# Loading the gate and up weights of a mixed decode kernel at the begin instead of the end

## The chip, the cores and the metric

The kernel runs on one core of one Trainium2 chip. The metric is device time in microseconds (us), the median of several runs. TensorE (PE) multiplies matrices and transposes, VectorE (DVE) and ScalarE (ACT) move and transform tiles, GpSimd (POOL) prepares constants, and SyncE (SP) issues nearly all of the DMAs.

## The reference

One decode step for four sequences, with two branches that a gate mixes:

```python
x = A_x                                                       # (4, 1, 512)
g = sigmoid((x * gate_w).sum(-1, keepdims=True))
# branch A: attention, 32 query heads, 8 key/value heads, head size 128, last 4096 positions
q = (x @ wq) as (4, 32, 1, 128)
scores = einsum("bhqd,bhkd->bhqk", q, k) * 128 ** -0.5        # k, v: last 4096 of 16384 positions
a = einsum("bhqk,bhkd->bhqd", softmax(scores), v) as (4, 1, 4096) @ wo
# branch B: a gated feed-forward of width 1792
gate = x @ W_gate;  up = x @ W_up
h = relu(gate) * up
b = h @ W_down
out = g * a + (1 - g) * b
```

Everything large is bf16. Per run the core reads 81.01 MB from HBM, almost all of it the windows of the key and value caches; the result is 4 KB.

## The kernel before

The attention is cut into `NSET = 8` sets; a set is one sequence and four of its eight key/value heads. Each set needs one block of keys (4096 KB, 32 KB in each of 128 partitions) and one block of values of the same size. `Ksb` and `Vsb` each have two slots, used in turn by even and odd sets. `Wbig` is a third buffer of 32 KB per partition.

Every engine's instructions are written down in order in a `Program`, with named events; a wait on an event becomes a semaphore wait ahead of the instruction. The order on each engine is thus set by hand, and nothing is rescheduled. SP's list is the order of the DMAs (lines 217 to 243). All are on SP's one queue, and the blocks land in the order of issue. A DMA that reuses a slot waits on SP until the last reader of the slot has finished, and everything behind it on SP waits too:

- wq into slot 1 of `Vsb` (line 533, issued ahead of the block), then K0, K1, V0, K2, V1, ..., K7, V6. K of set s waits for the scores of set s-2 (`SC`), V of set s for the products with V of set s-2 (`PV`; V1, into wq's slot, for an idle round).
- W_gate and W_up (1792 KB each, lines 230 and 232) into slot 0 of `Ksb`, which wait for the scores of set 6, the last reader of that slot. Then V7, which waits for `PV` of set 5.
- W_down (line 235) into slot 0 of `Vsb`, which waits for `PV` of set 6. Then wo into `Wbig` in five pieces (lines 240 and 243: 2048, 1280, 512 and twice 128 KB), with no wait of their own.

x and gate_w are small and come on ACT's queue (lines 224, 225).

PE's list: x is transposed (292), the gate's sum made (299), q = x @ wq (310) turned (328) and copied. A hardware loop then goes four times over two sets each. For a set, 64 transposes of K blocks (352) go through PSUM tile `TRT`; DVE (359) and ACT (357) copy them back over K. After five of the eight groups of transposes come the first half of the scores (373), after the rest the second half; DVE adds a mask and keeps the maximum (383). Then come the 64 products with V of the *previous* set (421), whose exponent (403, ACT) and transposition (413, DVE) ran beside this set's transposes.

Behind the loop stands the tail: the last set's maximum (390), exponent and transposition; `combine(0)` (440 to 448), which normalises the even sets; `gateup()` (453 to 474), that is 32 matmuls of x with W_gate and W_up into `TRT`, a ReLU on ACT and three operations on DVE, which make `hT`; the last set's 64 products with V; `combine(1)`; then 28 products of `hT` with W_down and 64 with wo, all accumulated in one PSUM tile (503), in the order in which the pieces of wo land; two copies (517, 518) and the DMA of the result (539).

## Time and profile before

| what | before |
|---|---|
| median of 3 runs | 196.43 us (196.17 to 196.50) |
| the profiled execution's own time | 196.16 us |
| its span in the profile | 194.9 us |
| bytes from HBM | 81.01 MB, 416 GB/s over the span |
| busy PE, PEld, DVE, ACT, POOL | 129.2, 101.0, 73.8, 66.5, 11.7 us |
| mean granted TensorE clock | 0.939 |

The profile is one execution, in microseconds from the span's start; 1.26 us of that execution lie outside the span. PE is TensorE's matmuls, PEld its weight loads, "SPq" the DMA issues of SP. L352 is line 352 of the kernel before. A timeline row gives start, duration, engine, line and operation, output<-input, count, and in brackets the idle time ahead of it with what ended it. A chain row gives start, duration, what. In rows with stretches of time, each engine's busy time and count is followed by the granted clock (1.00 is full), the busy share of the 16 DMA engines and GB/s.

### The profile page before, as it was taken

The numbers are of one execution on the slowest core, as the hardware profiler recorded it, in microseconds if no ns is written. First come the engines' busy times: TensorE is split into PE (matmuls) and PEld (weight loads), VectorE is DVE, ScalarE is ACT, GpSimd is POOL, SyncE is SP. The second block draws the span as 40 slices with busy tenths as digits, with TensorE's granted clock in tenths as the row PEclk, the third lists the DMA queues.
The fourth block names the chain that finished last, engine by engine and source line by source line (L and its number), as shares of the span: only waits on it lengthen the run. The fifth ranks groups of instructions, "written<-read, shape, count | busy, mean of one in ns | idle before, by whom it ended". The sixth has DMA issues, their size and how long they took to land.

```text
span 194.9 us, 3496 instructions
## 1 busy us (share of the span) xinstructions
PE 129.2 (66%) x1578; PEld 101.0 (52%) x1578; DVE 73.8 (38%) x95; ACT 66.5 (34%) x77; POOL 11.7 (6%) x43
## 2 busy tenths in 40 slices
PE   0137398788769649872887099649972987713964
PEld 0113396576556439651765097439651865503742
DVE  0200045259239323930682029324920492180000
ACT  2005025565255452435342424433435252510000
POOL 8820000000000000000000000000000000000000
PEclk9999999999999996999999859996999699995799
DMA  6999999999999999999999999999999999998992
GB/s 216 431 430 437 430 430 427 437 440 430 437 440 430 437 430 437 430 430 437 432 437 425 430 437 430 430 437 430 430 430 430 430 390 427 475 430 382 424 403 82
DMA packets 3881, 81.11 MB, mean 416 GB/s; under 512 B 409, under 2 KB 930, under 8 KB 1058
## 3 DMA queue, kind: packets, MB, share of 16 engines
q1 hardware_dynamic: 3864, 81.01, 97.3%
q8 instruction: 5, 0.08, 0.2%
q14 instruction: 2, 0.02, 0.0%
q10 hardware_dynamic: 10, 0.01, 0.0%
HBM read 81.01 MB, written 0.00 MB: 416 GB/s over the span
## 4 chain that ended last, share of the span: by engine, by line
DMA 59%; PE 21%; DVE 14%; ACT 3%; issue 1%; SPq 1%
DMA Ksb<-in_A_k_cache_dram 47%; PE TRT L352 15%; DMA Wbig<-in_A_wo_dram 12%; DVE Ksb L359 6%; DVE pT L413 5%; PE SCT L373 3%; DVE sc L383 3%; ACT Ksb L357 3%; PE OB L421 2%; PE SCT L503 1%; SPq L240 0%; PE FB L390 0%; SPq L533 0%; ACT outr L518 0%; SPq L235 0%
## 5 line engine op out<-in xcount | busy, mean ns | idle before, releaser
L352 PE MATMUL TRT<-identw,Ksb 128*128 128x128 f32 x512 | 75.1, 306 | 25.4 <-DMA Ksb<-in_A_k_cache_dram 17.5
L352 PEld LDWEIGHTS TRT<-identw,Ksb 128*128 128x128 f32 x512 | 65.9, 158 | 35.8 <-DMA Ksb<-in_A_k_cache_dram 18.8
L357 ACT COPY Ksb<-TRT 128x1024 f32<-128x1024 f32 x40 | 40.5, 1012 | 58.4 <-PE TRT L352 58.2
L359 DVE COPY Ksb<-TRT 128x1024 f32<-128x1024 f32 x24 | 29.4, 1223 | 40.1 <-PE TRT L352 40.1
L421 PE MATMUL OB<-Vsb,pT 128*32 128x256 bf16 x576 | 19.0, 288 | 7.5 <-DMA Vsb<-in_A_v_cache_dram 7.5
L373 PE MATMUL SCT<-Ksb,qS 128*32 128x512 bf16 x256 | 16.9, 381 | 8.8 <-ACT Ksb L357 8.8
L421 PEld LDWEIGHTS OB<-Vsb,pT 128*32 128x32 bf16 x576 | 16.4, 101 | 10.4 <-issue 7.9
L383 DVE CUSTOM_DVE_ANT_0 sc<-SCT,mask,mx 128x1024 bf16<-128x1024 f32 x8 | 10.3, 1284 | 26.9 <-PE SCT L373 26.9
L403 ACT ACTIVATE sc<-sc,negmax 128x2048 bf16<-128x2048 bf16 x8 | 16.0, 2002 | 10.7 <-DVE negmax L395 10.7
L413 DVE STREAM_TRANSPOSE pT<-sc 128x2048 bf16<-128x2048 bf16 x8 | 18.4, 2302 | 2.2 <-ACT sc L403 2.2
L430 ACT COPY osb<-OB 128x256 f32<-128x256 f32 x8 | 3.0, 372 | 31.1 <-PE OB L421 31.1
L373 PEld LDWEIGHTS SCT<-Ksb,qS 128*32 128x32 bf16 x256 | 5.2, 94 | 15.7 <-ACT Ksb L357 11.6
L383 DVE CUSTOM_DVE_ANT_0 sc<-SCT,mask 128x1024 bf16<-128x1024 f32 x8 | 9.8, 1225 | 2.2 <-PE SCT L373 2.2
L340 POOL COPY qS<-qW 128x64 bf16<-128x64 bf16 x8 | 1.8, 238 | 113.3 <-PE SCT L373 105.2
L390 PE MATMUL FB<-identw,mx 128*128 128x128 f32 x18 | 4.7, 343 | 5.7 <-issue 5.7
L395 DVE CUSTOM_DVE_ANT_0 mrow<-FB,qmask 128x128 f32<-128x128 f32 x8 | 2.3, 292 | 12.8 <-PE FB L390 12.8
L390 PEld LDWEIGHTS FB<-identw,mx 128*128 128x128 f32 x18 | 2.9, 200 | 7.6 <-issue 7.6
L292 PE MATMUL FB<-identw,xw 5*128 5x5 f32 x4 | 0.6, 262 | 8.5 <-POOL m L267 8.5
L503 PE MATMUL SCT<-Wbig,oq 128*4 128x256 bf16 x64 | 4.3, 273 | 2.6 <-DMA Wbig<-in_A_wo_dram 2.6
L310 PE MATMUL SCT<-Vsb,xT 128*32 128x512 bf16 x32 | 3.6, 631 | 2.8 <-DMA Vsb<-in_A_wq_dram 2.8
L292 PEld LDWEIGHTS FB<-identw,xw 5*128 5x128 f32 x4 | 0.6, 207 | 8.5 <-DVE xw L286 8.5
L503 PEld LDWEIGHTS SCT<-Wbig,oq 128*4 128x4 bf16 x64 | 2.7, 87 | 4.2 <-DMA Wbig<-in_A_wo_dram 3.6
(61 smaller groups left out, 42.7 us busy)
## 6 DMA issues: line engine op xcount, KB each, us to landing
Ksb<-in_A_k_cache_dram SPq DMA_DIRECT2D x8, 4096.0 KB, 24.2
Vsb<-in_A_v_cache_dram SPq DMA_DIRECT2D x8, 4096.0 KB, 32.2
Vsb<-in_A_wq_dram SPq DMA_DIRECT2D x1, 4096.0 KB, 12.3
Wbig<-in_A_wo_dram SPq DMA_DIRECT2D x1, 2048.0 KB, 21.5
Ksb<-in_B_W_gate_dram SPq DMA_DIRECT2D x1, 1792.0 KB, 19.7
Ksb<-in_B_W_up_dram SPq DMA_DIRECT2D x1, 1792.0 KB, 23.6
Vsb<-in_B_W_down_dram SPq DMA_DIRECT2D x1, 1792.0 KB, 17.0
Wbig<-in_A_wo_dram SPq DMA_DIRECT2D x1, 1280.0 KB, 24.1
```

Of the source, the lines that this page charges most:

```text
L310: P.op("pe", lambda e, half=half, t=t, g=g, col=col: e.matmul(SCT[32 * g:32 * g + 32, 512 * half:512 * half + 512], xT[:, t, :], Wq3[:, t, ...
L352: P.op("pe", lambda e, bk=bk, cc=cc, c=c: e.transpose(bk[:, cc * 128:(cc + 1) * 128], Kw[:, s % 2, c * 128:(c + 1) * 128], identw[:, :]), ...
L357: P.op("act", lambda e: e.copy(dst, bk), ("KTC", s, i), [("KT", s, i)], sem="va")
L359: P.op("dve", lambda e: e.tensor_copy(dst, bk), ("KTC", s, i), [("KT", s, i)], sem="vd")
L373: P.op("pe", lambda e, a=a, o=o, hb=hb, bank=bank: e.matmul(SCT[32 * a:32 * a + 32, 512 * hb:512 * hb + 512], qS[:, s % 2, o, :], k4[:, 16 ...
L383: P.op("dve", lambda e: e.tensor_tensor_reduce(sc[:, s % 2, pair * 1024:(pair + 1) * 1024], SCT[:, :], mask[:, :], 1.0, mx[:, s % 2, 0:1] ...
L390: P.op("pe", lambda e: e.matmul(FB[:, 384:512], mx[:, par, 1:2].to_broadcast([128, 128]), identw[:, :], start=True, stop=True), ("MT", s), ...
L403: P.op("act", lambda e: e.activation(sc[:, par, :], sc[:, par, :], ACTF.Exp, bias=negmax[:, par:par + 1], scale=SCALE, accum_out=rowsum[:, ...
L413: P.op("dve", lambda e: e.transpose(pT[:, par, :], sc[:, par, :]), ("PTT", s), [("EXP", s), ("PV", s - 2) if s >= 1 else None], sem="vd")
L421: P.op("pe", lambda e, g=g, blk=blk: e.matmul(OB[32 * g:32 * g + 32, 0:256], pT[:, par, 32 * blk:32 * blk + 32], Vsb[:, par, 256 * blk:256 ...
L430: P.op("act", lambda e: e.copy(osb[:, s, :], OB[:, 0:256]), ("OSB", s), [("PV", s)], sem="va")
L503: P.op("pe", lambda e: e.matmul(AB[32 * u:32 * u + 4, 0:256], stat, mov[:, 256 * u:256 * u + 256], start=start, stop=stop, tile_position=( ...
```

## The change

W_gate and W_up now go into `Wbig`, and wo into slot 0 of `Ksb`; `Wg`, `Wu` and `Wo3` name the new places.

- DMA order: W_gate takes the place ahead of the block that wq had, on a semaphore of its own; then come W_up, wq, K0, K1, V0 and so on. At the end V7 follows V6 directly, then W_down and the five pieces of wo. The pieces of wo have the scores of set 6 to wait for, an event that comes before the `PV` of set 6 for which W_down ahead of them waits.
- The 32 matmuls and four other operations of `gateup()` are written ahead of x @ wq, with W_gate's and W_up's waits separate. The first matmul of the loop's maximum waits for `hT` instead of x's transpose, and PE waits before the loop for the ReLU and the product, since the loop writes `TRT`.

Operations, sizes and pieces are the same.

```diff
-        Wg = Ksb[:, 0, 0:4 * FF].rearrange("p (t f) -> p t f", t=4)
-        Wu = Ksb[:, 0, 4 * FF:8 * FF].rearrange("p (t f) -> p t f", t=4)
+        Wg = Wbig[:, 0:4 * FF].rearrange("p (t f) -> p t f", t=4)
+        Wu = Wbig[:, 4 * FF:8 * FF].rearrange("p (t f) -> p t f", t=4)
...
-        Wo3 = Wbig[:, :].rearrange("p (i w) -> p i w", w=512)
+        Wo3 = Ksb[:, 0, :].rearrange("p (i w) -> p i w", w=512)
...
-        P.events[("V", -1)] = ("V1", 16, None, 0)
+        P.events[("WG",)] = ("wg", 16, None, 0)
...
+        P.dma("sp", lambda e: e.dma_start(Wbig[:, 4 * FF:8 * FF], B_W_up.rearrange("(p t) f -> p (t f)", p=128)), ("WU",))
+        P.dma("sp", lambda e: e.dma_start(Vsb[:, 1, :], A_wq.rearrange("(p t) w -> p (t w)", p=128)), ("V", -1), sem="V1")
         load_k(0)
         for s in range(1, NSET):
             load_k(s)
             load_v(s - 1)
-        P.dma("sp", lambda e: e.dma_start(Ksb[:, 0, 0:4 * FF], B_W_gate.rearrange("(p t) f -> p (t f)", p=128)),
-              ("WG",), [("SC", NSET - 2, NPAIR - 1)])
-        P.dma("sp", lambda e: e.dma_start(Ksb[:, 0, 4 * FF:8 * FF], B_W_up.rearrange("(p t) f -> p (t f)", p=128)),
-              ("WU",), [("SC", NSET - 2, NPAIR - 1)])
         load_v(NSET - 1)
...
-            P.dma("sp", lambda e, lo=lo, hi=hi: e.dma_start(Wbig[:, lo:hi], wo_src[:, lo:hi]), ("WO", k))
+            P.dma("sp", lambda e, lo=lo, hi=hi: e.dma_start(Ksb[:, 0, lo:hi], wo_src[:, lo:hi]), ("WO", k), [("SC", NSET - 2, 1)])
...
-                                                   wo_src3[:, WO_CUTS[-1]:32, 256 * u:256 * u + 256]), ("WOL", u))
+                                                   wo_src3[:, WO_CUTS[-1]:32, 256 * u:256 * u + 256]), ("WOL", u), [("SC", NSET - 2, 1)])
...
+        for t in range(4):
+            for which, W in ((0, Wg), (1, Wu)):
+                for g in range(4):
+                    P.op("pe", lambda e, which=which, W=W, t=t, g=g: e.matmul(
+                        TRT[32 * g:32 * g + 32, 512 * which:512 * which + FQ], xT[:, t, :], W[:, t, FQ * g:FQ * g + FQ],
+                        start=(t == 0), stop=(t == 3), tile_position=(0, 32 * g)),
+                        ("GU", which) if (t == 3 and g == 3) else None,
+                        [("WG",) if which == 0 else ("WU",), ("XTC",)])
...
-                 ("MT", s), [("SCC", s, 1)] if s >= 0 else [("XTC",)])
+                 ("MT", s), [("SCC", s, 1)] if s >= 0 else [("H",)])
...
-        def gateup():
...
+        P.op("pe", None, None, [("H0",), ("H1",)])
         for s in range(NSET):
...
         combine(0)
-        gateup()
         values(NSET - 1)
...
-        nc.sync.dma_start(Vsb[:, 1, :], A_wq.rearrange("(p t) w -> p (t w)", p=128)).then_inc(sems["V1"], 16)
+        nc.sync.dma_start(Wbig[:, 0:4 * FF], B_W_gate.rearrange("(p t) f -> p (t f)", p=128)).then_inc(sems["wg"], 16)
```

36 lines of the change are left out of this document (14 added, 22 removed).

## The prediction, made before the changed kernel was run

> **What bounds the kernel now.** I read the page's slices first, for the resource that is never idle:
>
> ```profile
> DMA  6999999999999999999999999999999999998992
> GB/s 216 431 430 437 430 430 427 437 440 430 437 440 430 437 430 437 430 430 437 432 437 425 430 437 430 430 437 430 430 430 430 430 390 427 475 430 382 424 403 82
> q1 hardware_dynamic: 3864, 81.01, 97.3%
> ```
>
> The 16 DMA engines are busy from the first slice (4.87 us each) to the last but one, at about 430 GB/s; the queue of the loads takes 97.3% of the span. The time is that of 81.01 MB in one queue, plus a head and a tail. Then the chain that ended last, for what follows the stream:
>
> ```profile
> 86.43 25.15 DMA Ksb<-in_A_k_cache_dram
> ...
> 126.19 24.25 DMA Ksb<-in_A_k_cache_dram
> ...
> 163.98 1.78 PE OB L421 x49
> ...
> 165.77 0.33 SPq L235
> ...
> 166.62 24.15 DMA Wbig<-in_A_wo_dram
> 190.81 2.38 PE SCT L503 x32
> ```
>
> K6 comes from 86.43+25.15 = 111.58, K7 from 150.44. The chain names W_down's and wo's issues (165.77, 166.14) because it goes back by semaphores; whether they were late is told by the backlog ahead of them. SP's timeline has the issues:
>
> ```profile
> 0.81 0.41 SPq L533 DMA_DIRECT2D Vsb<-in_A_wq_dram  x1
> ...
> 37.36 0.54 SPq L217 DMA_DIRECT2D Ksb<-in_A_k_cache_dram  x1
> ...
> 144.80 0.34 SPq L230 DMA_DIRECT2D Ksb<-in_B_W_gate_dram  x1
> 145.18 0.43 SPq L232 DMA_DIRECT2D Ksb<-in_B_W_up_dram  x1
> 146.54 0.55 SPq L221 DMA_DIRECT2D Vsb<-in_A_v_cache_dram  x1
> 165.77 0.33 SPq L235 DMA_DIRECT2D Vsb<-in_B_W_down_dram  x1
> 166.14 1.38 SPq L240 DMA_DIRECT2D Wbig<-in_A_wo_dram  x3
> ...
> 193.60 0.35 SPq L539 DMA_DIRECT2D out_dram<-outr  x1
> ```
>
> And the timeline of the compute engines from K7's landing on, to the last products:
>
> ```profile
> 150.48 5.42 PE L352 MATMUL TRT<-identw,Ksb 128*128 128x128 f32 x32 [3.57 <-DMA Ksb<-in_A_k_cache_dram]
> ...
> 163.81 1.92 PE L421 MATMUL OB<-Vsb,pT 128*32 128x256 bf16 x64
> ...
> 169.39 1.70 PE L457 MATMUL TRT<-Ksb,xT 128*32 128x448 bf16 x32
> ...
> 170.00 2.31 DVE L413 STREAM_TRANSPOSE pT<-sc 128x2048 bf16<-128x2048 bf16 x1 [2.16 <-ACT sc L403]
> 170.95 0.54 ACT L464 ACTIVATE hrelu<-TRT 128x448 f32<-128x448 f32 x1 [0.98 <-PE TRT L457]
> ...
> 172.81 0.89 DVE L466 TENSOR_TENSOR hrow<-TRT,hrelu 128x448 f32<-128x448 f32 x1
> ...
> 174.41 0.22 DVE L470 TENSOR_TENSOR hT<-hcol,gsb 128x56 bf16<-128x56 f32 x1
> ...
> 178.59 3.60 PE L421 MATMUL OB<-Vsb,pT 128*32 128x256 bf16 x64 [7.50 <-DMA Vsb<-in_A_v_cache_dram]
> ...
> 184.62 1.69 PE L503 MATMUL SCT<-Vsb,hT 128*4 128x256 bf16 x28
> ...
> 185.14 0.29 DVE L448 TENSOR_TENSOR oq<-TRT,rgate 64x128 bf16<-64x128 f32 x1
> 187.70 1.92 PE L503 MATMUL SCT<-Wbig,oq 128*4 128x256 bf16 x32 [1.39 <-DMA Wbig<-in_A_wo_dram]
> 190.81 2.37 PE L503 MATMUL SCT<-Wbig,oq 128*4 128x256 bf16 x32 [1.19 <-DMA Wbig<-in_A_wo_dram]
> ```
>
> To see: in the tail PE waits for each block of the stream in turn: V7 at 178.59, wo's first piece at 187.70, its second at 190.81. The last 32 products need 1.92 us (as the 32 before them did) and lie over 2.37: 0.45 us in them are waits for the last pieces. The end is set by the stream's last landing.
>
> **The change part by part.** *The same bytes in another order.* No DMA is added or removed. W_gate and W_up, 3584 KB = 3.67 MB, go from behind V6 to the front: at 430 GB/s all from wq to V6 lands 8.5 us later, and V7, W_down and wo, with the same bytes ahead of them as before, land when they did. In the sum: 0, if the queue never runs dry. The start stays as it is: the first issue is at 0.81 in both.
>
> *The calculation of gate and up at the begin.* What moves is 1.70 us of PE, 0.54 of ACT and, from 172.81 to 174.63, 1.8 of DVE.
>
> ```profile
> 9.79 0.16 DVE L297 COPY xT<-FB 128x16 bf16<-128x16 bf16 x1
> ...
> 13.12 3.60 PE L310 MATMUL SCT<-Vsb,xT 128*32 128x512 bf16 x32 [2.84 <-DMA Vsb<-in_A_wq_dram]
> ...
> 19.40 0.41 POOL L340 COPY qS<-qW 128x64 bf16<-128x64 bf16 x2 [8.12 <-DVE qW L334]
> 22.82 6.37 PEld L352 LDWEIGHTS TRT<-identw,Ksb 128*128 128x128 f32 x32 [3.65 <-DMA Ksb<-in_A_k_cache_dram]
> ```
>
> wq, 4096 KB, had landed at 13.12; the two weights, 512 KB less, are there at about 11.9, x's transpose at 9.95. The group takes 1.70 to 3.4 us on PE (doubled for a slow clock) and 2.4 behind it: ready by 17.7 at the latest. wq comes at 13.1+8.5 = 21.6, q is ready at 19.8+8.5 = 28.3, K0 comes at 31.3. Cover: 4 us ahead of wq. Were it gone (x comes behind the weights), q has 3.0 us up to K0, and behind that stands the backlog of the queue. Cost 0. In the tail it gains 0 as well: there the group lay between 169.39 and 174.63, while PE had V7 to wait for until 178.59.
>
> *The seam V7 to W_down.* This is the change's risk. W_down's issue waits for `PV` of set 6, at 165.77 before, and the five pieces of wo are queued on SP behind it. Before, W_gate, W_up and V7 were still to land then, V7 at 178.59: a cover of 12.8 us. Now K7 lands 8.5 us later, so do the scores and products behind it, and W_down is issued at 174.3, V7 still landing at 178.6: a cover of 4.3. Price of a DMA's start: the result's DMA, issued at 193.60, has begun and landed by the span's end at 194.9, 1.3 us. A precedent: K2 was issued at 37.36, when wq, K0, K1 and V0 had been issued, of which the last ends at 13.1+3×9.75 = 42.4; a cover of 5.0, and the slices about it (437, 440) show no gap. So 3 us are left over; set 7 would have to take 3 us longer. From K7's landing to the issue behind it, its set took 165.77−150.48 = 15.3; from a landing to the end of the scores one set took 126.19−111.58 = 14.6 (the scores release the next issue) and the last set 163.98−150.44 = 13.5, a spread of 1.1. Cost 0. wo's added wait costs nothing: the scores of set 6 are ahead of `PV` of set 6 on PE.
>
> V7 waits for `PV` of set 5, at 146.54+8.5 = 155.0, when V6 has until about 168.8 to land (V7's 178.6 less 9.75); no gap. W_down and wo are issued by 177.1 in all (174.3 and under 2.8 us for the six issues, the first four of which went from 165.77 to 167.52), ahead of their turn.
>
> *The tail on PE* starts 8.5 us later and loses `gateup`. pT of set 7 was ready at 172.31, now at 180.8, so the products with V7 start at 180.8, not at 178.59: from now on they wait for DVE. Before, from their start to W_down's products passed 184.62−178.59 = 6.03 us, 3.60 of it the products themselves, which ran at half clock; elsewhere the 64 take 1.92. The granted clock by stretches:
>
> ```profile
> 148.31:151.72 3.41, 1.24 (x11) 1.24 (x12) 0.11 (x1) 1.07 (x2) 0.00 (x0) 0.99 0.96 413
> 151.73:155.14 3.41, 3.41 (x18) 3.19 (x17) 1.35 (x2) 1.01 (x1) 0.00 (x0) 0.51 1.00 432
> ...
> 175.62:179.03 3.41, 0.44 (x12) 0.41 (x16) 0.00 (x0) 0.00 (x0) 0.00 (x0) 0.50 0.88 376
> 179.03:182.44 3.41, 3.16 (x60) 2.27 (x52) 0.00 (x0) 0.20 (x1) 0.00 (x0) 0.51 1.02 431
> ```
>
> Half clock (0.51) followed on a stretch in which PE was busy for 1.24 us of 3.41 as well as on one with 0.44. Now PE idles only from about 177.9 (169.39+8.5) to 180.8, 2.9 us. By the first of these rows that is enough for a slow stretch, by none is it sure: the products take 1.92 to 3.60. I take 3.60, the row of the same place. W_down's products start at 180.8+6.0 = 186.8 and end at 188.5 (fast: 186.8); wo's first 32 at 190.4 (fast: 189.6, as the piece lands at 187.7). The second piece lands at 190.8. PE is level again with 0.4 to 1.2 us in hand, plus the 0.45 of waits in the last group. `oq`, ready 6.8 us behind the start of the products (185.43−178.59), comes at 187.7 and delays nothing. Cost 0.
>
> The Trainium skill, "TensorE: Matmul & The Clock Gate", Part 1, states that PE falls to half rate after at least one idle window of about 3.4 us. By that, a pause of 2.9 us cannot fill a window, the products take 1.92, and wo's first 32 end at 189.6; by the trace's row at 148.31 a window only mostly idle is enough, and they end at 190.4. The predicted end is the same by both; by the page I would give the first rival below 8 in 100 instead of 15.
>
> *Sum:* 196.16 us of the profiled execution (span 194.9) and 0 for each part. The median of the runs stands 0.27 above that execution, and I give the median: **196.4 us**. The three runs lie within 0.33 us, 0.17%; about 0.2%, 0.4 us, is what can be told from no change.
>
> **The rivals.** *PE's tail becomes the bound (slower).* For it: the hand shrinks from a wait at every block to under a microsecond. It decides when wo's first products end behind 190.81+0.45 = 191.3: 0.9 us later than I have it. Set 7 at the long 14.6 (+1.1) gives 191.5 and 196.6; with W_down's products at half clock too (+1.7), 193.2, +1.9 and 198.3. Against it: in the last rows the clock was back after two stretches, and the row at 150.48 already has set 7 in a slow stretch. 15%, 196.6 to 198.3, say 197.3.
>
> *The seam runs dry (slower).* Decides from an issue of W_down later than 177.3 (178.6−1.3); every further us is one on the end. It takes a set 7 longer by 3 us, or a start of a DMA of over 4.3 us. 8%, 197 to 199.
>
> *The end of the stream shifts by itself (faster).* In the last 2 us the DMA engines are mostly done:
>
> ```profile
> 178.50:190.75 12.25, 9.17 (x142) 7.12 (x142) 0.64 (x3) 0.37 (x1) 0.00 (x0) 0.84 0.99 407
> 190.75:192.75 2.00, 1.94 (x30) 1.25 (x30) 0.00 (x0) 0.00 (x0) 0.00 (x0) 1.00 0.28 92
> ```
>
> A share of 0.28: a few engines lag behind the others and set the end. Were they level, the 0.18 MB would take 0.4 us rather than 2.0: up to 1.6 us, 194.8. Nothing in the change evens them out, except that smaller rows come first. 15%, about 195.7.
>
> *The tail relieved of gate and up (faster):* worth up to 1.7 us if PE set the end, 194.7; PE waited 7.5 us for V7 right behind the group. 2%.
>
> **How the numbers follow.** Forecast 60%, 195.9 to 196.9, of which 55% within 0.2% and the rest shared. The rivals: slower 15+8, faster 15+2. So faster 0.19, same 0.55, slower 0.26. The range of 195.5 to 197.6 leaves out the far ends of the rivals.
>
> **What would show it.** K7's wait on PE ends near 159.0 and V7's products wait for DVE's transposition at 180.8, not for the DMA. W_down is issued near 174.3 and no slice dips between 175 and 180; a dip there means the seam ran dry. wo's second piece still ends PE's wait near 190.8; if PE does not wait for it, the tail is the bound. The forecast is wrong if the lagging DMA engines end elsewhere, which moves the end though every step holds.

## The result: 0.7 to 0.8 per cent slower, and the profile after

| | before | after |
|---|---|---|
| median | 196.25 us (195.89 to 196.59, 12 runs) | 197.61 us (196.68 to 198.96, 12 runs) |
| ratio, 95% interval | | 1.0080 [1.0060, 1.0099] |
| profiled execution, span | 196.16, 194.9 us | 198.53, 197.3 us |
| last arrival of the loads in it | 192.75 | 194.94 |

The forecast was 196.4 with a range up to 197.6; the time lies just above it, and the most likely case, no change, is excluded. The times also spread over 2.3 us where those of before spread over 0.7. The profiled execution is a long one of these, 2.37 us over before's, where the medians differ by 1.36; the mechanisms are read in it, their sizes from the ratios.

The slices and queues of the page, for the kernel after:

```profile
DMA  6999999999999999999999999999999999989980
GB/s 204 430 476 425 432 452 415 425 425 432 415 425 425 435 438 438 445 425 445 420 434 432 425 425 425 438 425 425 438 432 445 432 432 425 445 358 404 407 347 20
...
q1 hardware_dynamic: 3864, 81.01, 96.4%
q8 instruction: 5, 0.08, 0.2%
```

The same 3864 packets and 81.01 MB. Slices 36 and 37 (172.6 to 182.5 us) have 358 and 404 GB/s where before has 430 and 382, 50 GB/s less in sum, and the last two are thinner (347 and 20 for 403 and 82). The timeline of SP:

```profile
156.67 0.53 SPq L221 DMA_DIRECT2D Vsb<-in_A_v_cache_dram  x1
175.19 0.33 SPq L233 DMA_DIRECT2D Vsb<-in_B_W_down_dram  x1
175.57 1.71 SPq L238 DMA_DIRECT2D Ksb<-in_A_wo_dram  x3
177.32 1.58 SPq L241 DMA_DIRECT2D Ksb<-in_A_wo_dram  x2
```

PE's timeline at the begin and in the tail (start, us, engine, line, what; in brackets the idle time ahead and what ended it):

```profile
12.63 2.81 PE L307 MATMUL TRT<-Wbig,xT 128*32 128x448 bf16 x28 [3.21 <-DMA Wbig<-in_B_W_up_dram]
...
159.77 5.62 PE L372 MATMUL TRT<-identw,Ksb 128*128 128x128 f32 x32 [2.73 <-DMA Ksb<-in_A_k_cache_dram]
...
173.23 1.92 PE L441 MATMUL OB<-Vsb,pT 128*32 128x256 bf16 x64
...
181.82 1.93 PE L441 MATMUL OB<-Vsb,pT 128*32 128x256 bf16 x64 [2.91 <-DVE pT L433]
...
186.18 1.69 PE L499 MATMUL SCT<-Vsb,hT 128*4 128x256 bf16 x28
189.91 2.78 PE L499 MATMUL SCT<-Ksb,oq 128*4 128x256 bf16 x32 [2.04 <-DMA Ksb<-in_A_wo_dram]
193.01 2.48 PE L499 MATMUL SCT<-Ksb,oq 128*4 128x256 bf16 x32 [0.33 <-DMA Ksb<-in_A_wo_dram]
```

And DVE's, the last operation of gate and up:

```profile
17.32 0.22 DVE L320 TENSOR_TENSOR hT<-hcol,gsb 128x56 bf16<-128x56 f32 x1
```

To see: the calculation of gate and up lies well hidden at the begin (hT at 17.5). The last products still wait for both pieces of wo, which come 2.2 us later than before (189.91 and 193.01 for 187.70 and 190.81). K7's wait ends 9.3 us later than before, not 8.5, and W_down is issued at 175.19. The loss is thus in the stream. The stretches of 2 us about that issue in before (busy us and count of PE, PEld, DVE, ACT, POOL; clock; DMA share; GB/s):

```profile
174.00:176.00 2.00, 0.00 (x0) 0.00 (x0) 0.60 (x2) 0.00 (x0) 0.00 (x0) 0.89 0.84 360
176.00:178.00 2.00, 0.00 (x0) 0.00 (x0) 0.00 (x0) 0.00 (x0) 0.00 (x0) 0.50 0.99 419
```

The same stretches in after:

```profile
174.00:176.00 2.00, 1.15 (x44) 0.85 (x32) 0.74 (x2) 0.37 (x1) 0.00 (x0) 1.00 0.84 360
176.00:178.00 2.00, 1.53 (x12) 1.42 (x13) 0.30 (x2) 0.68 (x1) 0.00 (x0) 1.00 0.85 299
```

Both have 360 GB/s up to 176; then before moves 419 and after 299. Such a row counts a packet whole in the stretch in which it begins, so it is rough. With each packet's bytes spread over the time that it took, after moves 0.27 MB less than before from 174 to 184 us, which is 0.63 us at 430 GB/s.

A finer reading comes from the single DMA packets of the trace. Every transfer has 16 completions, one from each of the 16 DMA engines when its share is done, so they tell how level the engines are. They arrive at the semaphore on which PE or SP waits about 0.4 us later. The table has the first transfer of each kernel (median and last of its 16 completions, and how many lie over 0.5 us behind the median), and the 16 arrivals of the last transfer (median, the last but one and the last), worked out from those records:

```
                         first transfer            last transfer's arrivals
                      first  median  last  late    median    15th    last
before                wq      12.48  12.72   0     191.26  192.72  192.75
after                 W_gate   7.08   7.97   4     192.19  193.77  194.94
after_again           W_gate   6.94   7.92   3     192.66  193.85  195.54
wo_ahead_of_down      W_gate   7.10   7.99   3     191.50  192.69  193.40
piece_ahead           W_gate   7.03   8.07   4     192.02  192.73  193.68
gate_first_up_late    W_gate   6.99   8.05   3     191.70  192.56  193.53
up_first_gate_late    W_up     7.00   8.08   1     191.26  192.63  192.70
gate_second_up_late   wq      12.51  12.71   0     191.28  192.77  192.80
wq_first              wq      12.38  12.75   0     192.23  192.76  193.65
wq_first_piece_ahead  wq      12.37  12.72   0     191.76  192.97  192.98
wq_first_wo_ahead     wq      12.41  12.68   0     191.24  192.66  192.67
wq_row_of_14k         14K wq   6.99   7.26   0     191.40  192.78  192.81
wq_into_third_buffer  wq      12.37  12.77   0     191.27  192.52  192.56
late_down_in_before   wq      12.48  12.71   0     191.56  192.78  193.18
late_turn_in_before   wq      12.35  12.70   0     191.22  192.52  192.58
```

(The other names are those of the experiments.) Two things show: after's engines are uneven from the first transfer on, and its last landing is late both in the middle (0.93 us) and more so at the last engine (2.19). A third is in the last two columns: in the profiles whose stream ends after 193 us, one engine alone is the last, 0.4 to 1.7 us behind the 15th; in the others these two are level, within 0.1 us.

### The profile page after: what moved, and what is told of

It is laid out like the page before. It is cut to its first block, busy times and chain, and to the rows that moved or that the text cites. A ratio compares the mean times of both kernels' runs of the same rounds, so it can differ in the third digit from the quotient of the medians.

```text
span 197.3 us, 3494 instructions
## 1 busy us (share of the span) xinstructions
PE 131.9 (67%) x1578; PEld 102.7 (52%) x1578; DVE 73.9 (37%) x95; ACT 66.5 (34%) x77; POOL 11.7 (6%) x43
## 3 DMA queue, kind: packets, MB, share of 16 engines
q1 hardware_dynamic: 3864, 81.01, 96.4%
HBM read 81.01 MB, written 0.00 MB: 411 GB/s over the span
## 4 chain that ended last, share of the span: by engine, by line
DMA 59%; PE 21%; DVE 14%; ACT 3%; issue 1%; SPq 1%
DMA Ksb<-in_A_k_cache_dram 51%; PE TRT L372 14%; DMA Ksb<-in_A_wo_dram 9%; DVE Ksb L379 6%; DVE pT L433 4%; PE SCT L393 3%; DVE sc L403 3%; ACT Ksb L377 3%; PE OB L441 2%; PE SCT L499 1%; SPq L227 0%; SPq L238 0%; PE FB L410 0%; SPq L529 0%; SPq L226 0%
## 5 line engine op out<-in xcount | busy, mean ns | idle before, releaser
L372 PE MATMUL TRT<-identw,Ksb 128*128 128x128 f32 x512 | 76.9, 312 | 23.9 <-DMA Ksb<-in_A_k_cache_dram 16.1
L372 PEld LDWEIGHTS TRT<-identw,Ksb 128*128 128x128 f32 x512 | 67.9, 162 | 34.0 <-DMA Ksb<-in_A_k_cache_dram 17.3
L441 PE MATMUL OB<-Vsb,pT 128*32 128x256 bf16 x576 | 17.3, 272 | 2.9 <-DVE pT L433 2.9
L441 PEld LDWEIGHTS OB<-Vsb,pT 128*32 128x32 bf16 x576 | 15.3, 96 | 5.1 <-DVE pT L433 3.0
L499 PE MATMUL SCT<-Ksb,oq 128*4 128x256 bf16 x64 | 5.3, 334 | 2.4 <-DMA Ksb<-in_A_wo_dram 2.4
L330 PEld LDWEIGHTS SCT<-Vsb,xT 128*32 128x32 bf16 x32 | 1.1, 140 | 9.3 <-DMA Vsb<-in_A_wq_dram 7.7
L499 PEld LDWEIGHTS SCT<-Ksb,oq 128*4 128x4 bf16 x64 | 3.2, 102 | 4.4 <-DMA Ksb<-in_A_wo_dram 3.2
L307 PE MATMUL TRT<-Wbig,xT 128*32 128x448 bf16 x32 | 3.4, 574 | 3.2 <-DMA Wbig<-in_B_W_up_dram 3.2
```

What stands on the lines that cost most here:

```text
L307: P.op("pe", lambda e, which=which, W=W, t=t, g=g: e.matmul(TRT[32 * g:32 * g + 32, 512 * which:512 * which + FQ], xT[:, t, :], W[:, t, FQ ...
L330: P.op("pe", lambda e, half=half, t=t, g=g, col=col: e.matmul(SCT[32 * g:32 * g + 32, 512 * half:512 * half + 512], xT[:, t, :], Wq3[:, t, ...
L372: P.op("pe", lambda e, bk=bk, cc=cc, c=c: e.transpose(bk[:, cc * 128:(cc + 1) * 128], Kw[:, s % 2, c * 128:(c + 1) * 128], identw[:, :]), ...
L441: P.op("pe", lambda e, g=g, blk=blk: e.matmul(OB[32 * g:32 * g + 32, 0:256], pT[:, par, 32 * blk:32 * blk + 32], Vsb[:, par, 256 * blk:256 ...
L499: P.op("pe", lambda e: e.matmul(AB[32 * u:32 * u + 4, 0:256], stat, mov[:, 256 * u:256 * u + 256], start=start, stop=stop, tile_position=( ...
```

## The experiments

Three theories: **the seam** (W_down is issued too near V7's end and the queue starts anew), **the start** (W_gate as the first transfer leaves engines behind which never catch up), **the tail** (PE begins set 7's products later and has no time in hand). Ratios are to the kernel before on the same chip.

**after_again.** The changed kernel once more, beside the others.

> The changed kernel once more, unchanged, as the yardstick of this group. Three theories of its extra 1.4 us. Seam: W_down, issued only some 3.4 us ahead of the end of what is queued, leaves DMA engines without work between V7 and W_down; then the slices at 175 to 179 us move less than 400 GB/s again. Spread: the 16 DMA engines end the queue further apart than before (a start in which small rows and x's small DMA come together, and instruction loads that hit an engine which is late already); then the last 2 us before the last landing have a low DMA share, as before, and the time differs from run to run by about 1 us. PE's tail: TensorE runs at half clock behind wo's pieces; then PE does not wait for wo's second piece. All three expect 197.1 to 198.7 us here.

197.72 us (196.30 to 199.04), 1.0068 [1.0043, 1.0094]. The slowdown repeats. PE's timeline has two differences from the first profile:

```profile
158.82 6.29 PE L372 MATMUL TRT<-identw,Ksb 128*128 128x128 f32 x32 [3.64 <-DMA Ksb<-in_A_k_cache_dram]
...
181.73 3.32 PE L441 MATMUL OB<-Vsb,pT 128*32 128x256 bf16 x64 [2.91 <-DVE pT L433]
```

K7's wait ends 8.3 us later than in before, not 9.3. There is the same pause of 2.91 us ahead of V7's products, but they take 3.32 us in place of 1.93.

**seam_in_before.** The kernel before, with W_down's issue made late.

```diff
-              ("WD",), [("PV", NSET - 2)])
+              ("WD",), [("PV", NSET - 2), ("H",)])
```

> The kernel before, in which the load of W_down (and wo's pieces behind it) waits for hT as well, which in the profile before is ready at 174.63 us: W_down is issued at about 174.7 instead of 165.8, 3.9 us ahead of V7's landing, as in the changed kernel. Nothing else moves. Seam theory: the stretch 175 to 179 us moves less, the end comes 0.5 to 1.5 us later, 196.8 to 197.8 us. Spread theory: the engines that are ahead run dry, but the last one has work until 178.3, so 196.3 us, as before. PE's tail: 196.3 us.

205.97 us, 1.0495 [1.0479, 1.0511]. It went further than meant: hT's signal goes to a semaphore kept for PE, and every other engine waits for DVE's next signal instead, which came behind the last set, as the timeline of SP shows:

```profile
184.91 0.33 SPq L235 DMA_DIRECT2D Vsb<-in_B_W_down_dram  x1
```

So it says nothing on the seam's size in the changed kernel, but it measures a start on an empty queue: the first packet of W_down starts at 185.87, 0.96 us behind the issue, the first one on some engines starts a microsecond after that, and these first packets take 0.54 to 1.33 us each. From V7's mean completion to W_down's it is 4.29 us where the queue is full; here W_down's mean completion, 191.30, lies 6.39 behind the issue. The difference, 2.1 us, is what a start costs a DMA engine that has run empty.

**late_down_in_before.** The same with an event that SP can read at once, the transposition of the gate's rows.

```diff
-              ("WD",), [("PV", NSET - 2)])
+              ("WD",), [("PV", NSET - 2), ("H2",)])
```

> The kernel before, with W_down's load waiting for the transposition of h (DVE, over at 174.39 us in the profile before) as well as for its slot, so that it is issued at about 174.4 us, 4.2 us ahead of V7's landing; in the changed kernel it was 175.2. Nothing else moves. The first try of this waited for a later event than meant, 184.9 us, and cost 9.8 us. Seam theory: W_down's first rows come late for the DMA engines that are ahead and slowly for all; a dip in the slices at 175 to 180 us, 196.8 to 197.5 us, and more difference from run to run. Start theory (the extra time comes from which engines are late from the begin): 196.2 us, as before.

196.61 us (196.24 to 198.27), 1.0034 [1.0016, 1.0053]. Its SP's timeline:

```profile
174.56 0.33 SPq L235 DMA_DIRECT2D Vsb<-in_B_W_down_dram  x1
```

Its stretch behind the issue, to be held against 419 GB/s in before:

```profile
176.00:178.00 2.00, 0.00 (x0) 0.00 (x0) 0.00 (x0) 0.00 (x0) 0.00 (x0) 0.50 0.87 329
```

Issued 4.1 us ahead of V7's landing at 178.65, with nothing else changed, the stream moves 0.12 MB less from 174 to 184 us (by the packets' times, as above), and its last arrival comes 0.43 us later. The seam alone costs, and at nearly the cover that I had counted as safe.

**down_6us_ahead_in_before.** The issue somewhat earlier.

```diff
-              ("WD",), [("PV", NSET - 2)])
+              ("WD",), [("PV", NSET - 2), ("RG", 0)])
```

> The kernel before, with W_down's load waiting for rgate of the even sets (DVE, over at 172.56 us in the profile before) as well: issued at about 172.6 us, 6.0 us ahead of V7's landing. Seam theory: 6 us are enough, no dip, 196.2 us; with 4.2 us it was 196.6 and uneven. If every wait added to W_down costs, whenever it ends: 196.6 us.

196.19 us, 1.0000 [0.9991, 1.0009]. The issue came later than planned, as SP's timeline has it:

```profile
173.71 0.33 SPq L235 DMA_DIRECT2D Vsb<-in_B_W_down_dram  x1
```

That is 4.9 us ahead of V7's landing, which PE's timeline shows:

```profile
178.62 3.61 PE L421 MATMUL OB<-Vsb,pT 128*32 128x256 bf16 x64 [6.48 <-DMA Vsb<-in_A_v_cache_dram]
```

Free at 4.9, not at 4.1. The records say why the step is so sharp. The engines finish V7 over 2 us, not together, and each that finishes ahead of "issue + 2.1" is held up until then. By that rule the mean loss per engine, against the one measured (W_down's mean completion behind V7's, less 4.29):

```
                         issue    V7 done,      loss by    loss
                                first    last   the rule  measured
down_6us_ahead_in_before 173.71 176.27  177.97    0.00     0.00
late_down_in_before      174.56 176.00  178.00    0.24     0.28
after                    175.19 175.80  178.65    0.57     0.68
wq_first                 175.39 175.95  178.01    0.90     0.82
after_again              175.13 175.91  177.75    0.56     1.22
```

The rule meets four of five; after_again lost twice as much as it gives, and I don't know why.

**wo_ahead_of_down** and **piece_ahead.** The changed kernel with the first piece of wo, which waits only for set 6's scores, ahead of W_down in the queue: 2048 KB, with its products ahead too; and 1024 KB with the order of the products unchanged.

```diff
-WO_CUTS = (0, 16, 26, 30)
+WO_CUTS = (0, 8, 16, 26, 30)
...
-        P.dma("sp", lambda e: e.dma_start(Vsb[:, 0, 0:NFT * 512], B_W_down.rearrange("(p i) w -> p (i w)", p=128)),
-              ("WD",), [("PV", NSET - 2)])
...
             P.dma("sp", lambda e, lo=lo, hi=hi: e.dma_start(Ksb[:, 0, lo:hi], wo_src[:, lo:hi]), ("WO", k), [("SC", NSET - 2, 1)])
+            if k == 0:
+                P.dma("sp", lambda e: e.dma_start(Vsb[:, 0, 0:NFT * 512], B_W_down.rearrange("(p i) w -> p (i w)", p=128)),
+                      ("WD",), [("PV", NSET - 2)])
```

(The first of the two keeps the old `WO_CUTS`.)

> The changed kernel with wo's first piece (2048 KB, it needs only the scores of set 6) loaded ahead of W_down, and its 32 products ahead of W_down's: 4.9 us more are queued behind V7 when W_down's wait ends. Seam theory: no dip at 175 to 179 us and the time of the kernel before, 196.2 us. Spread theory: unchanged from the changed kernel, 197.2 to 198.0 us. PE's tail: W_down's 28 products now stand behind wo's first 32 and end no earlier than 1.7 us behind 187.7 us, the tail is as tight as in the changed kernel, 197.2 to 198.0 us.

> The changed kernel with wo's first piece cut in two and its first half (1024 KB, 2.4 us of the queue) loaded ahead of W_down; the products stay in their order, so that PE's tail is as in the changed kernel. When W_down's wait ends, about 6 us are queued instead of 3.7. Seam theory: no dip at 176 to 180 us, 0.8 us back, 196.8 us; what is left over 196.2 is then the start. If the seam is all of it: 196.2 us. If the seam is nothing: 197.7 us.

196.92 us, 1.0038 [1.0026, 1.0051]; and 197.09 us, 1.0039 [1.0026, 1.0052]. In both profiles the engines go on behind V7 without a pause: the mean completion of the piece of wo lies 4.89 and 2.49 us behind V7's, about what 2048 and 1024 KB take at 430 GB/s. With the seam thus covered about half of the loss goes, though the intervals still overlap with after_again's, and the times draw together (196.82 to 197.04; 196.44 to 197.25). The other half stays, so the seam is not the whole.

**wq_first.** The changed kernel with wq first, and W_gate and W_up behind it; the matmuls in that order too.

```diff
-        nc.sync.dma_start(Wbig[:, 0:4 * FF], B_W_gate.rearrange("(p t) f -> p (t f)", p=128)).then_inc(sems["wg"], 16)
+        nc.sync.dma_start(Vsb[:, 1, :], A_wq.rearrange("(p t) w -> p (t w)", p=128)).then_inc(sems["V1"], 16)
...
+        P.dma("sp", lambda e: e.dma_start(Wbig[:, 0:4 * FF], B_W_gate.rearrange("(p t) f -> p (t f)", p=128)), ("WG",))
...
-        P.dma("sp", lambda e: e.dma_start(Vsb[:, 1, :], A_wq.rearrange("(p t) w -> p (t w)", p=128)), ("V", -1), sem="V1")
```

> The changed kernel with wq in its old place as the first load, W_gate and W_up right behind it, and their 32 matmuls behind x @ wq. The end of the queue is as in the changed kernel. Seam theory: 197.6 us, the dip stays. Spread theory, as far as it rests on the start with small rows: the engines start as in the kernel before, up to 0.8 us less spread, 196.6 to 197.0 us. PE's tail: 197.6 us.

196.90 us (196.23 to 198.21), 1.0035 [1.0018, 1.0052], against after's 1.0068 [1.0043, 1.0094] on the same chip; the intervals overlap a little.

**wq_first_piece_ahead** and **wq_first_wo_ahead.** That edit and one of the two above together.

> The same, with wq as the first load and W_gate and W_up behind it. Seam and start together: 196.2 us, narrow. If something in the tail of PE (products with V7 that wait for DVE, 3.2 us later than before) costs as well, it is left here: 196.6 us and more.

> The changed kernel with both cures: wq loaded first and W_gate and W_up behind it, and wo's first piece ahead of W_down. If the extra 1.5 us are the sum of a seam (0.8) and a start (0.7): 196.1 to 196.4 us, and narrow. If what is left lies in the tail (W_down's products behind wo's first ones): 196.9 us.

196.45 us, 1.0023 [1.0011, 1.0035]; and 196.94 us, 1.0040 [1.0025, 1.0054]. With the smaller piece ahead, start and seam are cured together and 0.2% stays. With the larger one the start's cure brought nothing (1.0040 for 1.0038), which the three theories do not explain. That piece moves products as well. The profile is of its shortest run, 196.20 us, with a stream that ends like before's (192.67); its long runs, up to 197.41, have none, and the cause stays open.

**wo_ahead_x_later.** wo_ahead_of_down with x's own small load held back until W_gate has landed, in case it disturbs the first transfer.

```diff
-        P.dma("act", lambda e: e.dma_start(xsb[0:4, :], A_x.rearrange("b o d -> (b o) d")), ("X",))
+        P.dma("act", lambda e: e.dma_start(xsb[0:4, :], A_x.rearrange("b o d -> (b o) d")), ("X",), [("WG",)])
```

> The changed kernel with wo's first piece ahead of W_down (196.92 us in the first group, no dip at the seam), and the two small loads of x and gate_w issued by ACT only when W_gate has landed, at about 6.5 us, so that they do not meet the engines' first rows. Start theory, as far as it is x's load: the 0.7 us that are left go, 196.2 to 196.4 us. If the small rows alone do it, or something else than the start: 196.9 us. Seam theory on its own says nothing of the rest.

197.26 us (196.05 to 198.26), 1.0048 [1.0028, 1.0069]: no gain, and 2 engines still lagged at the first transfer (8.16, median 7.56). They lag by 0.6 us, where 3 or 4 engines lag by up to 0.9 to 1.1 in the other kernels with W_gate first, so x's load may be a part of the cause but is not all of it.

**gate_first_up_late** and **gate_second_up_late.** These isolate the start. W_gate goes to the front and wo into the K slot as in the change, but W_up stays between V6 and V7 and the calculation stays in the tail, so only half of the bytes move: W_down is issued 7.5 and 8.5 us ahead of V7's landing. The two differ in one thing, whether W_gate is the first transfer or, behind wq, the second.

```diff
-        nc.sync.dma_start(Wbig[:, 0:4 * FF], B_W_gate.rearrange("(p t) f -> p (t f)", p=128)).then_inc(sems["wg"], 16)
+        nc.sync.dma_start(Vsb[:, 1, :], A_wq.rearrange("(p t) w -> p (t w)", p=128)).then_inc(sems["V1"], 16)
...
-        P.dma("sp", lambda e: e.dma_start(Vsb[:, 1, :], A_wq.rearrange("(p t) w -> p (t w)", p=128)), ("V", -1), sem="V1")
+        P.dma("sp", lambda e: e.dma_start(Wbig[:, 0:4 * FF], B_W_gate.rearrange("(p t) f -> p (t f)", p=128)), ("WG",))
```

> W_gate alone goes ahead of wq into the third buffer; W_up stays between V6 and V7, and the calculation of gate and up stays in the tail; wo goes into slot 0 of the keys. So only 1.84 MB are moved: W_down is issued near 170, 8 us ahead of V7's landing, and PE has its old tail nearly. If W_gate as the first transfer has a price of its own, 1.0015 to 1.003 (196.5 to 196.8), and the first transfer's completions spread over more than 1 us. If the start costs nothing, 0.9990 to 1.0010 (196.0 to 196.4).

> The same kernel as the one with W_gate alone moved, but wq is the first transfer and W_gate the second. Every other order, place and size is the same. By the theory of the first transfer, 0.9990 to 1.0010 (196.0 to 196.4), with the first transfer's completions within 0.6 us; by the theory that it is moving bytes ahead that costs, whatever comes first, the same ratio as with W_gate first.

W_gate first: 196.94 us (196.75 to 197.93), 1.0035 [1.0021, 1.0048]. W_gate second: 196.21 us (195.94 to 196.51), 0.9997 [0.9987, 1.0006]. The same work in the same buffers, one pair of transfers exchanged on one chip: the start is a cost by itself, 0.38%. The page's slices of the first:

```profile
GB/s 208 466 426 427 426 427 426 423 440 423 440 427 450 433 433 433 426 433 433 427 421 433 428 433 426 433 433 427 433 433 446 433 415 422 442 411 425 418 340 13
```

And of the second:

```profile
GB/s 223 430 420 487 430 430 430 427 430 427 430 430 427 430 430 430 430 430 430 430 432 430 425 430 430 430 430 437 430 430 430 430 437 415 459 430 402 417 403 77
```

No hole at the seam in either. The last transfer arrives at 193.53 and 192.80: the mean over the engines differs by only 0.19, the last by 0.73. PE's timeline of W_gate first shows what follows from it:

```profile
188.51 6.39 PE L502 MATMUL SCT<-Ksb,oq 128*4 128x256 bf16 x64 [4.03 <-DMA Ksb<-in_A_wo_dram]
```

The stretch of it in which these products run, with the granted clock 0.50:

```profile
190.75:192.75 2.00, 2.00 (x24) 1.21 (x20) 0.00 (x0) 0.00 (x0) 0.00 (x0) 0.50 0.35 109
```

The first piece of wo arrives from its last engine 0.7 us later (188.46 for 187.74), PE has stood for 4.03 us by then, and in that execution, which took 197.93 us, it does the last 64 products at half clock. The Trainium skill, "TensorE: Matmul & The Clock Gate", Part 1, has the rate fall to half after an idle window of about 3.4 us; this row agrees.

Where the 0.73 us come from is in the packets. On one engine they follow each other within 0.01 us, so that an engine can be followed through the trace. Up to W_down the last engine is no later with W_gate first than with W_gate second (182.13 and 182.33). Then, at 182.2 and 182.4, a block of instructions is loaded (the page's "q8 instruction") on one of the same engines, whose loads come about 1.5 us later from then on. With W_gate first the block falls to an engine that was late already (done with W_down at 181.55, 1.2 us behind the first engine), with W_gate second to one that was not (180.56, 0.3 us behind the first). The former is the one that is alone at the end. In after and after_again the block, at 185.56, falls to one of the last engines (done with W_down at 183.13 and 183.73), and wo's first piece arrives from it 1.5 and 1.7 us behind all others. By these traces the late engines cost what they do because the next instruction load hits one of them; no run moved that load, so this is read and not tested.

**What in the start it is.** Four kernels tried one property each of W_gate as the first transfer: halves of wq (rows of 16 KB); wq's first 14,336 bytes of each row as a transfer of its own (W_gate's row length); wq into the third buffer (W_gate's destination); W_up in W_gate's place.

```diff
-        nc.sync.dma_start(Vsb[:, 1, :], A_wq.rearrange("(p t) w -> p (t w)", p=128)).then_inc(sems["V1"], 16)
+        nc.sync.dma_start(Vsb[:, 1, 0:8192], A_wq.rearrange("(p t) w -> p (t w)", p=128)[:, 0:8192]).then_inc(sems["V1"], 16)
...
+        P.dma("sp", lambda e: e.dma_start(Vsb[:, 1, 8192:16384], A_wq.rearrange("(p t) w -> p (t w)", p=128)[:, 8192:16384]), ("WQB",))
```

for the halves in the kernel before, with 7168 for 8192 for W_gate's row length; for the other buffer, in before too (DVE fills slot 1 of the values with zeros for the idle round),

```diff
-        nc.sync.dma_start(Vsb[:, 1, :], A_wq.rearrange("(p t) w -> p (t w)", p=128)).then_inc(sems["V1"], 16)
+        nc.sync.dma_start(Wbig[:, :], A_wq.rearrange("(p t) w -> p (t w)", p=128)).then_inc(sems["V1"], 16)
```

and for W_up, in gate_first_up_late,

```diff
-        nc.sync.dma_start(Wbig[:, 0:4 * FF], B_W_gate.rearrange("(p t) f -> p (t f)", p=128)).then_inc(sems["wg"], 16)
+        nc.sync.dma_start(Wbig[:, 4 * FF:8 * FF], B_W_up.rearrange("(p t) f -> p (t f)", p=128)).then_inc(sems["wg"], 16)
```

> The kernel before, with wq loaded in two halves of 2048 KB (rows of 16 KB rather than 32 KB) at the begin; the end of the queue is untouched. Start theory, as far as it is the small rows of the first load: 196.6 to 197.0 us. Seam theory: 196.2 us.

> The kernel before with wq loaded as two DMAs, the first with 14,336 bytes of each row (W_gate's row length), the second with the other 18,432. If the late group of DMA engines at the start comes from the row length of the first transfer, its completions spread over 1.3 us or more as with W_gate, and the ratio is 1.0015 to 1.003. If it comes from something else (the matrix's place in memory, the buffer), the spread is within 0.6 us and the ratio 0.9990 to 1.0010.

> The kernel before with wq loaded first as ever, but into the third buffer (which wo takes at the end) instead of slot 1 of the values, which DVE fills with zeros at the start for the idle round. If the third buffer as the first destination makes the late group of DMA engines, the first transfer's completions spread over 1 us and the ratio is 1.002 to 1.005. If it is the matrix, they lie within 0.6 us and the ratio is 0.9990 to 1.0010.

> The kernel with W_gate alone moved to the front, with W_up in its place: W_up is the first transfer (the same row length, the same kind of matrix, another place in memory), W_gate stays between V6 and V7. If the price of the start belongs to the one matrix W_gate, the first transfer's completions lie within 0.6 us and the ratio is 0.9990 to 1.0010. If it belongs to any such matrix, or to the third buffer as the first destination, the spread is over 1 us and the ratio 1.002 to 1.005.

| | us | ratio | late engines |
|---|---|---|---|
| wq_in_halves | 196.27 | 1.0003 [0.9995, 1.0012] | 0 |
| wq_row_of_14k | 196.42 | 1.0007 [0.9998, 1.0016] | 0 |
| wq_into_third_buffer | 196.20 | 1.0002 [0.9993, 1.0010] | 0 |
| up_first_gate_late | 196.23 (195.98 to 197.88) | 1.0009 [0.9994, 1.0024] | 1 |

None brings the cost back. With W_up first one engine lagged by 1.1 us and one time of twelve, 197.88, was long; eleven were like before, and in the profile the block of instructions fell to another engine (15th and last arrival 192.63 and 192.70). So neither the row length nor the buffer does it alone, and W_gate's twin does it far less. Whether it is where W_gate lies in memory, no run here tells; nor whether rows that lie back to back there have a part in it, as W_gate's and W_up's do and those of the cut wq do not. The two runs with W_gate and with W_up first were on different chips, so the difference between these two is less sure than the one between W_gate first and second.

**late_turn_in_before.** The tail by itself: before, with set 7's exponents transposed five times over (the same result each time), so that V7's products start near 181.7 us, about when after's do.

```diff
+            late = 4 if s == NSET - 1 else 0
+            for n in range(late):
+                P.op("dve", lambda e: e.transpose(pT[:, par, :], sc[:, par, :]), ("PAD", n),
+                     [("EXP", s), ("PV", s - 2), ("PAD", n - 1) if n else None])
```

> The kernel before, in which DVE does the transposition of set 7 five times instead of once, so that the products with V7 start at about 181.7 us (181.8 in the changed kernel) and not at 178.6. DMAs are untouched. PE's tail theory: wo's pieces find PE behind, 0.3 to 1.5 us later than before, 196.5 to 197.7 us. Seam and start theories: 196.2 us, as the 3 us stand beside waits for wo.

196.30 us (195.99 to 197.14), 1.0017 [1.0005, 1.0030]; five of twelve lie at 196.8 to 197.1, the others near 196.2. PE's timeline, of the shortest run:

```profile
180.77 3.60 PE L425 MATMUL OB<-Vsb,pT 128*32 128x256 bf16 x64 [10.36 <-DVE pT L417]
184.86 2.48 PE L444 MATMUL TRT<-osb,Wsel 128*64 128x128 f32 x16 [0.48 <-ACT osb L434]
187.17 0.23 PE L447 MATMUL TRT<-rowsum,Wsum 128*64 128x4 f32 x2
187.33 1.69 PE L507 MATMUL SCT<-Vsb,hT 128*4 128x256 bf16 x28
188.85 4.16 PE L507 MATMUL SCT<-Wbig,oq 128*4 128x256 bf16 x64
```

V7's products start at 180.77, 1.0 us ahead of after's, so this tests most of the delay and not all of it. From 188.85 the 64 products with wo run without a wait, though the stream ended as early as in before (192.58). PE is level with the stream: in this profile it costs nothing, and a slow stretch more has no reserve to go into. That the five long runs have such a stretch is not shown by a profile, but it fits that their mean granted clock is 0.887 to 0.904, and that of the seven others 0.912 to 0.930.

**seam_and_tail_in_before.** Both of these edits together, to see whether they add.

> The kernel before with the two late things together: W_down's DMA also waits for hT's transposition (issue near 174.4, as the changed kernel has it), and set 7's exponents are transposed five times over (products with V7 start near 180.8). wq stays first. If the seam (1.0034 alone) and PE's tail (1.0017 alone) add and the start has a share of its own in the changed kernel, 1.004 to 1.006 (197.0 to 197.4). If the changed kernel's 1.0068 to 1.008 comes from seam and tail alone and they amplify each other, 1.0065 to 1.008 (197.5 to 197.8). If one covers the other, 1.003 to 1.004 (196.8 to 197.0).

205.66 us, 1.0475 [1.0450, 1.0500], and no answer: the gate's transposition stands behind set 7's on DVE, so W_down waited for all five of those, as DVE's timeline shows:

```profile
179.29 2.31 DVE L417 STREAM_TRANSPOSE pT<-sc 128x2048 bf16<-128x2048 bf16 x1
...
183.05 0.65 DVE L473 STREAM_TRANSPOSE hcol<-hrow 128x448 f32<-128x448 f32 x1
```

SP's timeline has the issue behind it:

```profile
183.79 0.33 SPq L235 DMA_DIRECT2D Vsb<-in_B_W_down_dram  x1
```

It does give a second reading of a start on an empty queue: W_down's mean completion, 190.06, lies 6.27 us behind the issue, 2.0 more than 4.29.

That the three add thus rests on their sizes: 0.34% (late_down_in_before), 0.38% (W_gate first against second) and 0.17% (late_turn_in_before) make 0.89%, against 0.68 and 0.80 measured for the change. Taken away from the change in turn, the seam gives 0.29% back (1.0068 to 1.0039), the start 0.33 (1.0068 to 1.0035), both 0.45, and 0.23 is left. Both together thus give back less than the two one by one (0.62). These were not all measured on one chip, and the intervals reach 0.1 to 0.3% to each side, so that the shares add is argued from their sizes and not shown.

## Why the prediction was wrong, step by step

*"The same bytes in another order": cost 0.* The 8.5 us were right in the middle: K7's wait ended 9.3 us later in the first profile and 8.3 in the second (158.82). The sentence that failed is "The start stays as it is". I compared the times of the first issues and not what the first transfer does to the engines: with W_gate first, 2 to 4 of the 16 finish it late, the last 0.6 to 1.1 us behind the median, in all six profiles that have it, with wq first none. In a queue that never pauses, an engine that is late stays late: from W_gate to W_up the sixteen lags of after are the same within 0.01 us. By the traces the time is lost where the instruction load of the tail then hits such an engine. Cost about 0.35%, not 0.

*"The calculation of gate and up at the begin": cost 0.* Right at both ends: hT at 17.5, wq's products at 22.35, no time back in the tail.

*"The seam V7 to W_down": cost 0.* This step failed, and more by its yardstick than its numbers; the sign that I had named for it, a dip between 175 and 180 us, was there. I had the issue at 174.3; it came at 175.19 in the first profile and 175.13 in the second. But late_down_in_before, issued at 174.56, lost time with nothing else changed. Two inputs were wrong together. The price of a start was taken from the result's small DMA, 1.3 us; on an empty queue W_down's takes 2.1 us. The cover was counted to V7's landing, which is the *last* engine's end (178.6); the first is done at 175.8 to 176.3, and the row of the DMA share, 0.28 in the last 2 us, which I quoted for another rival, said that they end apart. The precedent, K2 with a cover of 5.0 us, was sound but lay on the free side: 4.9 is free, 4.1 is not. The rival "The seam runs dry" had the mechanism and the time (197 to 199), but a threshold of 177.3 in place of about 174 (V7's first engine done at 176.05, less 2.1), and so 8% in place of the larger share. The Trainium skill, "DMA: Bandwidth & Descriptors", section "Latency and other measured facts", gives about 0.6 us to the first byte of such a queue; here the first packet started 0.96 us behind the issue, and late and slow first packets on the other engines make the 2.1.

*"The tail on PE": cost 0.* V7's products did wait for DVE, at 181.82 for the 180.8 foreseen. In the first profile that is mostly K7's landing; in the second K7 came as foreseen and its set took 1.1 us longer (181.73 less 158.82 is 22.9, where 172.31 less 150.48 was 21.8). The products took 1.93 us in four profiles (after, wo_ahead_of_down, wo_ahead_x_later, wq_first_wo_ahead) and 3.28 to 3.51 in four (after_again, wq_first, piece_ahead, wq_first_piece_ahead), all behind the same pause of 2.91 us. So both of the readings that I weighed happen; the rule of the Trainium skill, "TensorE: Matmul & The Clock Gate", Part 1, by which such a pause, under about 3.4 us, costs nothing, meets four of the eight. I booked 0 on a reserve of 0.4 to 1.2 us; late_turn_in_before measures 0.17% for most of the delay. In the profiles of after PE still waits for wo's second piece, so the rival "PE's tail becomes the bound" names what can be a part of the loss, not its main cause.

*"The end of the stream shifts by itself"* was put down as a gain. It was the right place, the engines that lag and set the end, with the wrong sign: the median of the last transfer's arrivals came 0.93 us later, the last one 2.19.

*The sum.* Three zeros made 0: the start's was not examined, the seam's stood on a cover counted to the wrong end, the tail's on 0.4 to 1.2 us. Their measured sizes are each near what a measurement can tell, and together they are not. The base was a little high as well: the median of three runs was 196.43, that of twelve is 196.25.

## What to carry to other kernels

When one queue carries everything, count the cover of the next issue from the moment when the *first* DMA engine runs out of work, and against the price of a start of a large transfer on an empty queue (2.1 us here), not from the landing, which is the last engine's. A transfer whose buffer is free early, queued ahead of one that must wait, buys the cover back (piece_ahead). And moving a load to the front of a saturated queue is a change in itself: look at how level the engines leave the first transfer, and at the engine that the next instruction load hits. Only a pause evened them out here: in wq_first the sixteen completions of V7 lie 2.1 us apart, and those of W_down, behind the gap, 1.1.

## What the runs showed of the hardware that was not expected

*An instruction load costs one DMA engine about 1.5 us for good.* The page's "q8 instruction" row has 5 packets of 16 KB per run; in before they come at 31.9, 42.6, 54.9, 182.6 and 191.9 us and take 0.93 to 1.07. Behind each of the first three, the engine that carried it, followed from packet to packet, is 1.5 us later against the other engines than it was before, and stays so. The two blocks of 8 KB on "q14 instruction" (93.9 and 104.6) cost their engines 0.7 and 0.9. By all five, the sixteen completions go from 0.5 us apart (12.21 to 12.72) to 1.9 (176.05 to 177.94). The Trainium skill, "Runtime: NRT & Kernel Launch", section "Instruction fetch mechanics", has blocks of 16 KB on a DMA queue of their own, mostly hidden; the size agrees, but in a queue that sets the time they are not hidden. In after such a load at 185.6 was followed by wo's first piece arriving, from its last engine, at 189.87 where the mean is 187.19.

*One transfer differs from its twin as the first one.* W_gate first left 2 to 4 engines behind in six of six profiles, W_up one engine in one, wq none in any; with wq neither the row length nor the buffer did it, x's load is at most a part, and the cause stays open.

*A thin queue slows single packets.* The first packets of W_down take 0.54 us each when it is queued early, and up to 1.25 to 1.71 when it is issued into a queue that is running out (late_down_in_before, after, wq_first).
